# Windowed attention and a gated feed-forward on one core: third tile's units moved, second weight block rebuilt in order of use, first weights behind first transposes

## The chip, the core and the metric

The kernel runs on one core of one Trainium2 chip. The metric is the device time of one execution in microseconds (us). The core's engines work side by side, each through its own row of instructions in order: TensorE (PE for matmuls, PEld for the loading of their stationary operand), VectorE (DVE), ScalarE (ACT), GpSimd (POOL), and SyncE (SP), which here only issues DMAs. They wait for each other by semaphores.

## The reference

```python
pos = np.arange(S)
rel = pos[:, None] - pos[None, :]
mask = (rel >= 0) & (rel < 64)
scores = np.where(mask, q @ k.T / sqrt(D), -1e9)
attn = softmax(scores)
x = heads_side_by_side(attn @ v)
gate = 1.0 / (1.0 + np.exp(-(x @ w_gate)))
val = x @ w_val
out = (gate * val) @ w_out
```

This is the reference in short. Batch 8, 8 heads, 576 positions, head size 64, so 4608 tokens of 512 features; the hidden layer has 1536 features. q, k and v are float32; the three weights come as 64-bit floats and are handed in as 64-bit integers.

## The kernel before, in words

**Tiles.** The tokens are cut into 12 tiles of 384 (`TT`), taken as pairs. An attention *unit* is one tile and one pair of heads, `(t, p)`, and has three stages: `stage_a` (scores s by 24 small matmuls on TensorE, L200; the masked row minimum on VectorE, L218; exponentials on ScalarE, L227; the row sums' reciprocals on VectorE, L233 and L234; the multiplication by them on GpSimd, L236), `stage_b` (transposes pp on TensorE, L244, copied to pT by ScalarE, L249) and `stage_c` (oo = attention times v, L261). A name such as s0_2_0 is half 0 of tile 2, heads pair 0.

**Weights.** A weight block j (128 hidden features) has three pieces: m = 0 gate, m = 1 value, m = 2 output; the piece's number is i = 3j + m. Each is fetched as 64-bit words (`raw`, `conv_load`, L99) and rebuilt: `conv_a` on ScalarE (L111 writes w32, L112 the low part), `conv_b` on VectorE (L120 zz, L122, L124), and `conv_c`, which splits it in two parts whose sum carries nearly all bits, by a cast on ScalarE (L143) and a subtraction on VectorE (L144). Pieces 0 and 1 of a block are also stored to DRAM: w32 itself (w32d, L137) and its parts (wd, L397), for later pairs of tiles. There are 6 buffers for raw, 3 for w32 (`W32`), 7 for the split pieces (`WB`).

**The first pair of tiles.** Tiles 0 and 1 go through the feed-forward directly: ph = up-projection (`up`, L296, 12 matmuls each, gate and value), a sigmoid on ScalarE (L317), the product h and its split on VectorE, and y = down-projection (`down`, L360, 9 matmuls per block of tile 0). Names: ph1_0_2 is the value half (1) of tile 0 in block 2; w1_2 is the piece m = 1 of block 2. During it the units of tiles 2 and 3 are slipped in. Later pairs use a product scheme with seven block products (`product`, L451) and weights read back from DRAM; the change leaves these stages as they are.

**What sets the order.** Python code gives every step a planned time (`put`) and sorts by it (L642); a scheduler then places the instructions on the engines. TensorE keeps the sorted order (`pe`, `keep_in_program_order`). `tc.issue_after` keeps an instruction behind another in the scheduler's order. Exponentials and sigmoids use two different tables of ScalarE; `table_order` chains them in the planned order. `plan` (L532 and on) lists up and down steps of the first pair; position i of it gets, from `fill`, the stages of units: a unit's scores half a position past its start, its transposes some three positions later, its oo at the next start. Before, the starts are 1, 6, 11, 16, ... Conversions get their times at L579, and their `issue_after` marks at L645 to L652.

Of the kernel before, what the change touches and what calls it, by code (L numbers as in the profile page):

```python
# [26 lines left out]
def attn_ffn(ctx: ExitStack, tc: tile.TileContext, qT, kT, vN, w_gate, w_val, w_out, out):  # L27


    nc = tc.nc  # L30
# [4 lines left out]
    NP = DM // P  # L35
# [23 lines left out]
    for key in ((0, 0), (1, 0), (0, 1)):  # L59
        m = const.tile([P, P], F32, name=f"m_{key[0]}{key[1]}")  # L60
        nc.gpsimd.memset(m, 0.0)
        for h in range(2):
            rows = slice(h * BLK, (h + 1) * BLK)
            nc.gpsimd.affine_select(out=m[rows], in_=m[rows], pattern=[[1, P]], compare_op=ALU.is_ge,
                                    fill=NEG, base=-1, channel_multiplier=-1)
            nc.gpsimd.affine_select(out=m[rows], in_=m[rows], pattern=[[-1, P]], compare_op=ALU.is_ge,
                                    fill=NEG, base=BLK, channel_multiplier=1)
            if key[h]:
                nc.gpsimd.affine_select(out=m[rows], in_=m[rows], pattern=[[1, P]], compare_op=ALU.is_ge,
                                        fill=NEG, base=-BLK, channel_multiplier=0)  # L70
# [8 lines left out]
    marks = {"pT": {}}  # L79
# [46 lines left out]
    def conv_c(i):  # L126
        j, m = divmod(i, KINDS)
        _, w32 = conv.pop(i)
        tag, bufs = ("W", WB) if m < 2 else (f"wo_{j}", 1)
        w2 = wts.tile([P, 2, DM], F32R, name=f"w{m}_{j}", tag=tag, bufs=bufs)  # L130
        hi, lo = w2[:, 0, :], w2[:, 1, :]
        split(w32, hi, lo, nc.vector)
        if m == 2:
            wo[j] = (hi, lo)
        else:
            wgv[m][j] = (hi, lo)
            nc.sync.dma_start(out=w32d[m][j], in_=w32)  # L137
            H = DM // 2
            for name, half in (("A11", 0), ("A12", 1)) if j < NK else (("A22", 1),):
                put_part(m, j % NK, name, w2[:, :, half * H:(half + 1) * H])  # L140

    def split(w32, hi, lo, eng):
        nc.scalar.copy(hi, w32)  # L143
        eng.tensor_sub(out=lo, in0=w32, in1=hi.bitcast(F32))  # L144

# [246 lines left out]
    def put_part(m, k, name, parts):  # L394
        n = [w for w, _, _ in PRODUCTS].index(name)
        q, half = divmod(NPR * m + n, 2)
        nc.sync.dma_start(out=wd[k][q][:, half], in_=parts.bitcast(F32))  # L397

    def w_sums(m, k):
        H = DM // 2  # L400
        a1, a2 = [mp.tile([P, DM], F32, name=f"a{i}_{m}_{k}", tag="w32", bufs=W32) for i in range(2)]
        nc.sync.dma_start(out=a1, in_=w32d[m][k])
        nc.sync.dma_start(out=a2, in_=w32d[m][k + NK])
        sw = mp.tile([P, 4, H], F32, name=f"sw_{m}_{k}", tag="raw", bufs=RAW)
        nc.gpsimd.tensor_add(out=sw[:, 0, :], in0=a2[:, :H], in1=a2[:, H:])
        nc.gpsimd.tensor_sub(out=sw[:, 1, :], in0=sw[:, 0, :], in1=a1[:, :H])
        nc.gpsimd.tensor_sub(out=sw[:, 2, :], in0=a1[:, :H], in1=a2[:, :H])
        nc.gpsimd.tensor_sub(out=sw[:, 3, :], in0=a1[:, H:], in1=sw[:, 1, :])
        for i in range(0, 4, 2):
            w2 = wts.tile([P, 2, 2, H], F32R, name=f"ws{i}_{m}_{k}", tag="W", bufs=WB)  # L410
            split(sw[:, i:i + 2, :], w2[:, 0], w2[:, 1], nc.gpsimd)
            for e in range(2):
                put_part(m, k, f"S{i + e + 1}", w2[:, :, e, :])
# [90 lines left out]
    def put(tm, o, f, *a):  # L504
        events.append((tm, o, f, a))
# [24 lines left out]
    def unit(s, n):  # L530
        return 2 * s + n // 2 % 2, n // 4 + n % 2 * 2

    plan, fill = [], {}
# [5 lines left out]
        if n < NF:  # L539
            plan.append(("up", 1, n))  # L540
    at, now = {}, 0.0
    for n in range(2 * NP):
        i = 1 + 5 * n
        fill.setdefault(i + 0.5 + (i < len(plan) and plan[i][0] == "down"), []).append((0, *unit(1, n)))
        late = 0.5 if i + 3 < len(plan) and plan[i + 3][0] == "up" else 1
        for f, d in ((1, 3 + late), (2, 5)):
            fill.setdefault(i + d, []).append((f, *unit(1, n)))

    def attend(i):
        nonlocal now  # L550
# [25 lines left out]
            now = 0.0  # L576
    for i in range(KINDS * NF):
        j, m = divmod(i, KINDS)
        tm = at[("up", 0, max(j, 1))] + ((-10, -2, 10 * j - 5) if j < 2 else (-14, -12, 2))[m]  # L579
        if i < 2:  # L580
            tm = A0 + 11 + 8 * i
        else:
            put(tm - (30 if j == 0 or j == 1 and m < 2 else 6), 2.5, conv_load, i)
        put(tm, 1, conv_a, i)
        put(tm + 2.4, 2, conv_b, i)
        put(tm + 2.5, 2, conv_c, i)
# [20 lines left out]
    for s in range(1, NS):  # L607
        a, b = 2 * s, 2 * s + 1
# [11 lines left out]
        for k in range(NK):  # L620
# [5 lines left out]
            for m in range(2):  # L626
                for n in range(NPR):
                    put(now, 9, product, s, k, m, n)
                    now += PRT
                    if n in (2, 4, 6) and len(downs) > (RESERVE if m else 0) * (k == 1):  # L630
                        j, x = downs.pop(0)
# [11 lines left out]
    for _, _, f, a in events:  # L643
        if f in (conv_a, conv_b, conv_c):
            with ExitStack() as behind:  # L645
                j, m = divmod(a[0], KINDS)
                key = j - AHEAD if m < 2 else j - 1
                early = ("1_2",) if a[0] == 3 else ("1_3",) if a[0] in (2, 4) else (key, "1_3")
                for ins in [i for nm in early for i in marks.get(nm, ())]:
                    behind.enter_context(tc.issue_after(ins))  # L650
                f(*a)
        else:  # L652
            f(*a)
# [43 lines left out]
```

## Time and profile before

| what | us |
|---|---|
| median of 3 runs (1025.39 to 1027.74) | 1027.52 |
| the profiled execution | 1027.02 |
| its span, first to last instruction | 1025.2 |
| PE busy, share of the span | 987.4, 96% |
| DVE busy | 661.5, 65% |
| ACT busy | 525.8, 51% |
| POOL busy | 264.2, 26% |
| granted TensorE clock, mean | 0.997 |

Times in rows of the profile count from the span's start. A row of the timeline has the start, the duration, the engine, the source line, the operation with what it writes and reads (numbers left out), how many it merges, and in brackets how long its engine was idle before it and what ended that. A row of the stretches has for each engine the busy time and the number of instructions, then the granted TensorE clock (1.00 is full speed), the share of the 16 DMA engines and GB/s. A source line of the kernel after is one higher than before from L144 on, and further on by up to four.

### The profile page before, as it was taken

The numbers are of one execution on the slowest core, as the hardware profiler recorded it, in microseconds if no ns is written. First come the engines' busy times: TensorE is split into PE (matmuls) and PEld (weight loads), VectorE is DVE, ScalarE is ACT, GpSimd is POOL, SyncE is SP. The second block draws the span as 40 slices with busy tenths as digits, with TensorE's granted clock in tenths as the row PEclk, the third lists the DMA queues.
The fourth block names the chain that finished last, engine by engine and source line by source line (L and its number), as shares of the span: only waits on it lengthen the run. The fifth ranks groups of instructions, "written<-read, shape, count | busy, mean of one in ns | idle before, by whom it ended". The sixth has DMA issues, their size and how long they took to land.

```text
span 1025.2 us, 19858 instructions
## 1 busy us (share of the span) xinstructions
PE 987.4 (96%) x6984; PEld 883.3 (86%) x6984; DVE 661.5 (65%) x1810; ACT 525.8 (51%) x1409; POOL 264.2 (26%) x287
## 2 busy tenths in 40 slices
PE   6869999998999999999999999999999999999998
PEld 4769999887799888989988989988989988999996
DVE  6878987736676765766665766676666677344532
ACT  6967876736565445544453654454555544311122
POOL 4200101676762241122122221213212124010100
PEclk9989999999999999999999999999999999999999
DMA  9799985989999723767651776761777662466500
GB/s 301 276 312 332 305 301 187 333 301 336 380 323 317 223 96 127 236 211 221 206 184 47 239 230 205 220 203 40 226 221 214 209 194 73 138 221 203 188 31 32
DMA packets 126244, 221.51 MB, mean 216 GB/s; under 512 B 9409, under 2 KB 82625, under 8 KB 126145
## 3 DMA queue, kind: packets, MB, share of 16 engines
q1 hardware_dynamic: 126144, 220.24, 65.9%
q8 instruction: 56, 0.92, 0.4%
q14 instruction: 44, 0.35, 0.1%
HBM read 178.52 MB, written 41.68 MB: 215 GB/s over the span
## 4 chain that ended last, share of the span: by engine, by line
PE 76%; DMA 6%; DVE 6%; ACT 5%; POOL 3%; issue 3%; SPq 0%; POOLq 0%; DVEq 0%; ACTq 0%
PE pr L451 40%; PE y L360 24%; PE ph L296 5%; PE oo L261 3%; PE s L200 3%; PE pp L244 2%; ACT p L227 2%; DVE w L124 1%; POOL ws L144 1%; DMA out_dram<-yo 1%; DVE w L122 1%; DMA raw<-in_moe_w_gate_dram 1%; DVE p L218 1%; DMA k<-in_kT_dram 1%; ACT raw L112 1%
## 5 line engine op out<-in xcount | busy, mean ns | idle before, releaser
L451 PE MATMUL pr<-x_T,wt 128*128 128x384 f32 x1440 | 288.7, 340 | 5.1 <-DVE c L457 2.8
L451 PEld LDWEIGHTS pr<-x_T,wt 128*128 128x128 f32 x1440 | 251.0, 188 | 21.4 <-DVE u L457 5.4
L360 PE MATMUL y<-w,hh 128*128 128x512 f32 x804 | 250.4, 392 | 0.0
L451 PE MATMUL pr<-x_B,wt 128*128 128x384 f32 x1080 | 221.0, 341 | 0.2
L451 PEld LDWEIGHTS pr<-x_B,wt 128*128 128x128 f32 x1080 | 187.9, 188 | 7.9 <-ACT g L306 1.3
L236 POOL TENSOR_TENSOR p<-p,rs 128x384 f32<-128x384 f32 x92 | 78.5, 855 | 407.9 <-DVE rs L234 374.6
L360 PEld LDWEIGHTS y<-w,hh 128*128 128x128 f32 x804 | 148.7, 188 | 21.4 <-ACT hh L325 1.4
L360 PE MATMUL y<-w,hl 128*128 128x512 f32 x402 | 158.6, 394 | 0.6 <-DVE hl L329 0.6
L457 DVE TENSOR_TENSOR u<-pr,p 128x384 f32<-128x384 f32 x120 | 66.7, 556 | 132.0 <-PE pr L451 128.1
L227 ACT ACTIVATE p<-p,mn 128x128 f32<-128x128 f32 x288 | 110.5, 393 | 75.6 <-DVE mn L218 75.4
L329 POOL TENSOR_TENSOR hl<-h,hh 128x384 fp32r<-128x384 f32 x60 | 64.6, 1077 | 239.9 <-DVE hh L327 229.3
L296 PE MATMUL ph<-x,w 128*128 128x384 f32 x576 | 110.3, 344 | 8.5 <-ACT w L143 7.2
L296 PEld LDWEIGHTS ph<-x,w 128*128 128x128 f32 x576 | 100.9, 191 | 12.5 <-ACT w L143 7.8
L360 PEld LDWEIGHTS y<-w,hl 128*128 128x128 f32 x402 | 75.4, 188 | 19.5 <-DVE hl L329 3.3
L218 DVE CUSTOM_DVE_ANT_0 p<-s,m 128x128 f32<-128x128 f32 x288 | 65.3, 286 | 34.9 <-PE s L200 29.3
L462 ACT COPY p<-pr 128x384 f32<-128x384 f32 x60 | 28.4, 473 | 90.5 <-PE pr L451 76.7
L457 DVE TENSOR_TENSOR c<-pr,u 128x384 f32<-128x384 f32 x120 | 66.7, 556 | 12.1 <-PE pr L451 5.8
L249 ACT COPY pT<-pp 128x384 f32<-128x384 f32 x96 | 42.0, 481 | 49.0 <-PE pp L244 48.9
L329 DVE TENSOR_TENSOR hl<-hb,hh 128x384 fp32r<-128x384 f32 x60 | 39.1, 663 | 40.5 <-ACT hh L325 40.1
L310 DVE SCALAR_TENSOR_TENSOR g<-g,e 128x384 f32<-128x384 f32 x96 | 53.3, 567 | 8.0 <-ACT e L307 5.6
L261 PEld LDWEIGHTS oo<-pT,v 128*64 128x64 f32 x1152 | 39.2, 139 | 21.0 <-ACT pT L249 11.4
L325 ACT CAST hh<-hb 128x384 fp32r<-128x384 f32 x60 | 30.0, 512 | 51.6 <-PE y L360 51.4
(73 smaller groups left out, 1221.2 us busy)
## 6 DMA issues: line engine op xcount, KB each, us to landing
wt<-wd SPq DMA_DIRECT2D x210, 512.0 KB, 4.3
v<-in_vN_dram SPq DMA_DIRECT2D x48, 384.0 KB, 4.5
wd<-ws SPq DMA_DIRECT2D x48, 256.0 KB, 4.9
k<-in_kT_dram SPq DMA_DIRECT2D x48, 224.0 KB, 4.1
q<-in_qT_dram SPq DMA_DIRECT2D x48, 192.0 KB, 4.0
wd<-w SPq DMA_DIRECT2D x36, 256.0 KB, 6.2
out_dram<-yo SPq DMA_DIRECT2D x36, 256.0 KB, 2.1
raw<-in_moe_w_gate_dram SPq DMA_DIRECT2D x12, 512.0 KB, 4.6
```

Source lines behind the costliest of these rows:

```text
L200: pe(nc.tensor.matmul(sc[h][half * BLK:(half + 1) * BLK, u, :], qt[h * BLK:(h + 1) * BLK, U * BLK:(U + 1) * BLK], kt[h * BLK:(h + 1) * BLK ...
L218: nc.vector.tensor_tensor_reduce(out=pt[:, u, :], in0=sc[h][:, u, :], in1=masks[key], op0=ALU.add, op1=ALU.min, scale=-SCALE, scalar=3.0e3 ...
L227: exp = nc.scalar.activation(pt[:, u, :], pt[:, u, :], AF.Exp, bias=mn[:, u:u + 1], scale=-1.0, **sums)
L236: eng.tensor_mul(out=pt, in0=pt, in1=rs.unsqueeze(2).broadcast_to([P, UP, P]))
L249: cp = nc.scalar.copy(pT, pp)
L261: pe(nc.tensor.matmul(oo[h * BLK:(h + 1) * BLK, U * BLK:(U + 1) * BLK], vt[:, U, h * BLK:(h + 1) * BLK], pT[h][:, U // 2, half * BLK:(half ...
L296: pe(nc.tensor.matmul(ph, l, r, start=i == 0, stop=i == len(prs) - 1))
L310: nc.vector.scalar_tensor_tensor(out=g, in0=g, scalar=1.0, in1=e, op0=ALU.add, op1=ALU.mult)
L329: return eng.tensor_sub(out=h_lo, in0=h32, in1=h_hi.bitcast(F32))
L360: pe(nc.tensor.matmul(yb[y], l, r, start=first and n == 0, stop=last and n == 2))
L451: pe(nc.tensor.matmul(ps, l, r, start=new and i == 0, stop=i == len(prs) - 1, skip_group_check=not new))
L457: nc.vector.tensor_add(out=o, in0=ps, in1=a)
```

## The change

```diff
-        split(w32, hi, lo, nc.vector)
+        marks[("w", i)] = (split(w32, hi, lo, nc.vector),)
...
     def split(w32, hi, lo, eng):
-        nc.scalar.copy(hi, w32)
+        cp = nc.scalar.copy(hi, w32)
         eng.tensor_sub(out=lo, in0=w32, in1=hi.bitcast(F32))
+        return cp.ins
...
-    for n in range(2 * NP):
-        i = 1 + 5 * n
-        fill.setdefault(i + 0.5 + (i < len(plan) and plan[i][0] == "down"), []).append((0, *unit(1, n)))
-        late = 0.5 if i + 3 < len(plan) and plan[i + 3][0] == "up" else 1
-        for f, d in ((1, 3 + late), (2, 5)):
-            fill.setdefault(i + d, []).append((f, *unit(1, n)))
+    starts = (4, 8, 13, 17, 22, 26, 31, 36, 41)
+    for n, (i, nxt) in enumerate(zip(starts, starts[1:])):
+        late = 0 if nxt < i + 5 else 0.5 if i + 3 < len(plan) and plan[i + 3][0] == "up" else 1
+        for f, x in ((0, i + 0.5), (1, i + 3 + late), (2, nxt)):
+            fill.setdefault(x, []).append((f, *unit(1, n)))
...
-        tm = at[("up", 0, max(j, 1))] + ((-10, -2, 10 * j - 5) if j < 2 else (-14, -12, 2))[m]
+        tm = at[("up", 0, max(j, 1))] + ((-10, -2, 6 * j - 0.5) if j < 2 else (-9, -8, 2) if j == 2 else (-14, -12, 2))[m]
...
-                early = ("1_2",) if a[0] == 3 else ("1_3",) if a[0] in (2, 4) else (key, "1_3")
+                early = {3: ("1_2",), 2: ("1_3",), 4: ("1_3",), 5: ("1_3",)}.get(a[0], (key,))
+                if j == 2 and m < 2:
+                    early += tuple(("w", i) for i in (3, 4))
                 for ins in [i for nm in early for i in marks.get(nm, ())]:
                     behind.enter_context(tc.issue_after(ins))
+                if a[0] < 2:
+                    behind.enter_context(tc.issue_after(marks["pT"][a[0]]))
```

Three things move. The units of tiles 2 and 3 with heads pairs 0 and 2, which are the first four slipped in, start at plan positions 4, 8, 13 and 17 instead of 1, 6, 11 and 16; the first and the third of them have their transposes half a position nearer behind their scores than the others. Block 2's gate and value pieces stand behind the casts of block 1's, so that block 1 (w0_1, w1_1) is rebuilt first, then w2_0, then block 2. And the first two pieces (w0_0, w1_0) are rebuilt only behind the copies of the first and the second unit's transposes. No instruction is added or taken away.

ScalarE at the program's start, before (p are exponentials, pT the copies of transposes, w32, raw and w the steps of a weight piece):

```order
L227 ACTIVATE p0_0_1_305,rs0_0_1_307<-p0_0_1_305,mn0_0_1_306 128x128 x3
L111 ACTIVATE w32_0_0_399<-raw_0_0_224 128x512
L112 ACTIVATE raw_0_0_224<-raw_0_0_224 128x512
L227 ACTIVATE p1_0_1_317<-p1_0_1_317,mn1_0_1_318 128x128 x3
L249 COPY pT0_0_0_352<-pp0_0_0_348 128x384
L143 CAST w0_0_424<-w32_0_0_399 128x512
L249 COPY pT1_0_0_358<-pp1_0_0_354 128x384
L227 ACTIVATE p0_0_2_360,rs0_0_2_362<-p0_0_2_360,mn0_0_2_361 128x128 x3
L227 ACTIVATE p1_0_2_372<-p1_0_2_372,mn1_0_2_373 128x128 x3
L111 ACTIVATE w32_1_0_548<-raw_1_0_233 128x512
```

and of the kernel after:

```order
L228 ACTIVATE p0_0_1_305,rs0_0_1_307<-p0_0_1_305,mn0_0_1_306 128x128 x3
L228 ACTIVATE p1_0_1_317<-p1_0_1_317,mn1_0_1_318 128x128 x3
L250 COPY pT0_0_0_350<-pp0_0_0_346 128x384
L250 COPY pT1_0_0_356<-pp1_0_0_352 128x384
L228 ACTIVATE p0_0_2_358,rs0_0_2_360<-p0_0_2_358,mn0_0_2_359 128x128 x3
L228 ACTIVATE p1_0_2_370<-p1_0_2_370,mn1_0_2_371 128x128 x3
L111 ACTIVATE w32_0_0_397<-raw_0_0_224 128x512
L112 ACTIVATE raw_0_0_224<-raw_0_0_224 128x512
L273 CAST x_0_0_415<-oo_0_0_402 128x384
L250 COPY pT0_0_1_434<-pp0_0_1_430 128x384
L143 CAST w0_0_422<-w32_0_0_397 128x512
L250 COPY pT1_0_1_440<-pp1_0_1_436 128x384
```

The three steps of w0_0 that stood ahead of and between the copies pT0_0_0 and pT1_0_0 now follow the exponentials of the third unit; the cast of w0_0 stands between the copies of the second unit.

ScalarE at the second block, before, from the exponentials of the unit (2, 0) to the cast of w1_1:

```order
L227 ACTIVATE p0_2_0_909,rs0_2_0_911<-p0_2_0_909,mn0_2_0_910 128x128 x3
L227 ACTIVATE p1_2_0_921,rs1_2_0_923<-p1_2_0_921,mn1_2_0_922 128x128 x3
L143 CAST w0_2_976<-w32_0_2_933 128x512
L111 ACTIVATE w32_1_1_964<-raw_1_1_418 128x512
L111 ACTIVATE w32_1_2_969<-raw_1_2_875 128x512
L317 ACT_TABLE_LOAD
L317 ACTIVATE g_0_1_995<-ph0_0_1_982 128x384
L112 ACTIVATE raw_0_3_1036<-raw_0_3_1036 128x512
L112 ACTIVATE raw_1_3_1053<-raw_1_3_1053 128x512
L111 ACTIVATE w32_2_1_1046<-raw_2_1_967 128x512
L112 ACTIVATE raw_2_2_1070<-raw_2_2_1070 128x512
L143 CAST w1_1_1001<-w32_1_1_964 128x512
```

and after, from the first step of w1_1 on:

```order
L111 ACTIVATE w32_1_1_907<-raw_1_1_400 128x512
L112 ACTIVATE raw_1_1_400<-raw_1_1_400 128x512
L111 ACTIVATE w32_2_0_912<-raw_2_0_428 128x512
L112 ACTIVATE raw_2_0_428<-raw_2_0_428 128x512
L112 ACTIVATE raw_2_1_910<-raw_2_1_910 128x512
L318 ACTIVATE g_1_0_880<-ph0_1_0_867 128x384
L143 CAST w0_1_845<-w32_0_1_838 128x512
L143 CAST w1_1_940<-w32_1_1_907 128x512
L112 ACTIVATE raw_0_2_882<-raw_0_2_882 128x512
L112 ACTIVATE raw_1_2_884<-raw_1_2_884 128x512
L143 CAST w2_0_950<-w32_2_0_912 128x512
L111 ACTIVATE w32_0_2_972<-raw_0_2_882 128x512
```

The two steps of w1_1 now stand ahead of w2_0's and the gate g_1_0, its cast right behind w0_1's; the table loads and the exponentials of the unit have left this place, and block 2's w32 steps follow w2_0's cast.

TensorE from the up half ph0_1_0 to the transposes of the unit (2, 0), one row or two of each step, before:

```order
L296 MATMUL ph0_1_0_877<-x_1_3_862,w0_0_424 128x384 x3
L200 MATMUL s0_2_0_895<-k_2_0_839,q_2_0_838 64x128
L200 MATMUL s1_2_0_896<-k_2_0_839,q_2_0_838 64x128
...
L296 MATMUL ph1_1_0_943<-x_1_3_862,w1_0_583 128x384 x3
L296 MATMUL ph0_0_1_982<-x_0_0_415,w0_1_869 128x384 x3
...
L296 MATMUL ph1_0_1_1017<-x_0_0_415,w1_1_1001 128x384 x3
...
L360 MATMUL y_0_2_1049<-w2_0_940,hl_0_0_807 128x512
L296 MATMUL ph0_1_1_1055<-x_1_0_708,w0_1_869 128x384 x3
...
L244 MATMUL pp0_2_0_1079<-ident_81,p0_2_0_909 128x128 x3
L244 MATMUL pp1_2_0_1085<-ident_81,p1_2_0_921 128x128 x3
L296 MATMUL ph1_1_1_1091<-x_1_0_708,w1_1_1001 128x384 x3
```

and after:

```order
L297 MATMUL ph0_1_0_867<-x_1_3_864,w0_0_422 128x384 x3
L297 MATMUL ph1_1_0_886<-x_1_0_708,w1_0_583 128x384 x3
...
L297 MATMUL ph0_0_1_915<-x_0_0_415,w0_1_845 128x384 x3
...
L361 MATMUL y_0_2_1001<-w2_0_950,hl_0_0_807 128x512
L297 MATMUL ph0_1_1_1017<-x_1_0_708,w0_1_845 128x384 x3
...
L201 MATMUL s0_2_0_1041<-k_2_0_935,q_2_0_934 64x128
L201 MATMUL s1_2_0_1042<-k_2_0_935,q_2_0_934 64x128
...
L297 MATMUL ph1_1_1_1079<-x_1_0_708,w1_1_940 128x384 x3
...
L361 MATMUL y_0_2_1001<-w2_1_1038,hl_0_1_969 128x512
L245 MATMUL pp0_2_0_1183<-ident_81,p0_2_0_1055 128x128 x3
L245 MATMUL pp1_2_0_1189<-ident_81,p1_2_0_1067 128x128 x3
```

The scores s_2_0 moved from behind ph0_1_0 to behind ph0_1_1, past four up halves and a y; the transposes pp moved from behind ph0_1_1 to behind the y of block 1.

## The prediction

> **What bounds the kernel now.** I read the page first, then busy time by stretch, then TensorE's waits, then the timelines of the engines around the one large gap. TensorE leads:
>
> ```profile
> PE 987.4 (96%) x6984; PEld 883.3 (86%) x6984; DVE 661.5 (65%) x1810; ACT 525.8 (51%) x1409; POOL 264.2 (26%) x287
> ```
>
> So 1025.2 - 987.4 = 37.8 us without a matmul is all that any reordering can win, beside matmuls that ran slowly. By stretch (columns: us, busy us and instructions of PE, PEld, DVE, ACT, POOL, then granted clock, DMA share, GB/s), the one big gap lies between 52 and 61 us, and the clock is granted at half speed just behind it:
>
> ```profile
> 52.00:61.00 9.00, 2.18 (x11) 1.86 (x12) 7.72 (x17) 8.92 (x24) 2.19 (x2) 0.89 0.91 301
> 61.00:62.00 1.00, 0.80 (x3) 0.29 (x3) 1.00 (x3) 0.37 (x1) 0.00 (x0) 0.50 1.09 262
> 62.00:66.00 4.00, 4.00 (x12) 3.91 (x13) 2.24 (x4) 2.11 (x4) 0.00 (x0) 0.52 0.88 263
> ```
>
> TensorE's timeline through it (L200 scores, L296 up-projection; the y rows are L360, from the chain in order of time; the bracket is the idle time before the row and what ended it):
>
> ```profile
> 46.79 0.89 PE L200 MATMUL s<-k,q 64*64 64x128 f32 x24
> 47.60 2.38 PE L296 MATMUL ph<-x,w 128*128 128x384 f32 x12
> 50.34 0.62 PE L296 MATMUL ph<-x,w 128*128 128x384 f32 x2 [0.35 <-ACT w L143]
> 51.94 2.01 PE L296 MATMUL ph<-x,w 128*128 128x384 f32 x10 [0.98 <-DVE w L144]
> 60.77 1.01 PE L296 MATMUL ph<-x,w 128*128 128x384 f32 x2 [6.82 <-ACT w L143]
> 61.98 3.57 PE L296 MATMUL ph<-x,w 128*128 128x384 f32 x10 [0.20 <-DVE w L144]
> 70.34 6.50 PE L296 MATMUL ph<-x,w 128*128 128x384 f32 x36
> 116.43 0.91 PE L261 MATMUL oo<-pT,v 128*64 128x64 f32 x22 [0.47 <-ACT pT L249]
> ```
>
> ```profile
> 65.55 2.29 PE y L360 x9
> 89.34 2.08 PE y L360 x9
> ```
>
> The rows before order print name them: s_2_0, ph1_1_0, ph0_0_1 (waits for w0_1, 0.35 and 0.98 us), ph1_0_1 (waits for w1_1, 6.82 and 0.20 us), y of block 0. From 62 us on TensorE hardly stops: the 0.47 us of the last row are its only wait until 180 us. The 6.82 us are w1_1's place in ScalarE's row: its conversion starts behind a table load, six exponentials, w0_2, and behind it another table load and a gate stand before its cast:
>
> ```profile
> 50.83 1.28 ACT L227 ACT_TABLE_LOAD   x1
> 52.12 0.40 ACT L227 ACTIVATE p<-p,mn 128x128 f32<-128x128 f32 x1
> 54.95 1.23 ACT L111 ACTIVATE w<-raw 128x512 f32<-128x512 f32 x2
> 56.20 1.28 ACT L317 ACT_TABLE_LOAD   x1
> 60.10 1.27 ACT L143 CAST w<-w 128x512 fp32r<-128x512 f32 x2
> ```
>
> **The second block in order of use.** I replay ScalarE and VectorE from 45 us with the durations of these rows, in the times of the profile before:
>
> ```profile
> 45.35 0.68 ACT L111 ACTIVATE w<-raw 128x512 f32<-128x512 f32 x1
> 49.31 0.47 ACT L317 ACTIVATE g<-ph 128x384 f32<-128x384 f32 x1
> 47.05 2.36 ACT L112 ACTIVATE raw<-raw 128x512 int32<-128x512 uint32 x4
> 46.10 0.68 DVE L124 CUSTOM_DVE_ANT_0 w<-raw,w 128x1024 uint16<-128x1024 uint16 x1
> 46.70 0.91 DVE L120 TENSOR_SCALAR zz<-w 128x512 int32<-128x512 int32 x2
> 47.52 1.29 DVE L122 SCALAR_TENSOR_TENSOR w<-w,zz 128x512 int32<-128x512 int32 x2
> 51.20 0.69 DVE L144 TENSOR_TENSOR w<-w,w 128x512 fp32r<-128x512 f32 x1
> 51.80 0.55 DVE L335 TENSOR_TENSOR h<-ph,g 128x384 f32<-128x384 f32 x1
> ```
>
> Start to start, zz costs 0.41, L122 0.60, L124 0.60, L144 about 0.60, h 0.47; on ScalarE L111 and L112 0.57 each, a cast 0.52. ScalarE from 45.35: w32_1_1, raw_1_1, w32_2_0, raw_2_0, raw_2_1 end at 48.2; gate g_1_0 at 48.7; cast of w0_1 at 49.2. VectorE from 46.70: two zz, two L122, two L124, h32_1_0, then w0_1's subtraction: 0.82 + 1.20 + 1.20 + 0.47 + 0.60 = 4.3, so 51.0, and 51.1 with a semaphore; w1_1's follows at 51.6, w2_0's (a cast of hh between) at 52.6.
>
> TensorE: s_2_0 (0.81, start to start) is gone from here, so ph1_1_0 ends at 49.99 - 0.81 = 49.18. The first two matmuls of ph0_0_1 end at 49.8; it waits 1.3 us for 51.1, then 2.01 to 53.1; ph1_0_1 finds w1_1 ready, 6.50 / 3 = 2.17 to 55.3; y finds w2_0 ready, 2.08 to 57.4. Before, y ended at 65.55 + 2.29 = 67.84: 10.4 us earlier, less the 0.8 of scores that come later: **-9.6 us**. As a check by kind: waits 8.35 to 1.3 give 7.05; slow clock gives 3.57 - 2.01, 1.01 - 0.62 and 2.29 - 2.08 = 2.16; one restart less gives 0.46.
>
> The clock part rests on the rows at 0.50 and 0.52, about 5 us long after a wait of 6.82 us, while the wait of 0.98 us left its ten matmuls at 2.01. So the new wait of 1.3 us should cost no clock. The Trainium skill, "TensorE: Matmul & The Clock Gate", Part 1, says that an idle window of about 3.4 us drops the clock to half and that about 3.4 us of work restore it; by that the slow clock would cost 1.7 us, not 2.16, and the sum would be 0.5 us smaller. The trace's stretch at half clock is longer than the page's, and I use the trace.
>
> **The third tile's units, later.** The four moved units keep all their work: no instruction is added, the table loads stay 18 in ScalarE's row. What can newly be late is the first unit. Its scores now start close behind the second block, at about 59.6, and stand three up halves and one y ahead of pp_2_0 (3 x 2.17 + 2.08 = 8.6 us), while ScalarE puts two weight steps between its two halves. The nearest unit of before, and the stores on which a w32 buffer waits (3 buffers, L106):
>
> ```profile
> 81.99 0.89 PE L200 MATMUL s<-k,q 64*64 64x128 f32 x24
> 89.24 0.83 POOL L236 TENSOR_TENSOR p<-p,rs 128x384 f32<-128x384 f32 x1 [0.74 <-DVE rs L234]
> 91.26 0.82 PE L244 MATMUL pp<-ident,p 128*128 128x128 f32 x6
> L137 SPq DMA_DIRECT2D w32d<-w x16: 319/327/362, 24.1 to 119.5; - x16
> DMA to landing us min/median/max: 2.1/3.8/8.1
> 55.00 2.19 POOL L236 TENSOR_TENSOR p<-p,rs 128x384 f32<-128x384 f32 x2 [14.71 <-DVE rs L234]
> ```
>
> There the second multiplication ended at 90.07, 1.2 us before it was needed. Now: w32_1_2 waits for the store of w32_1_1 (issued at 49.5, landed 3.8 later, 53.3), is written at 53.9, and VectorE's zz, two L122 and one L124 finish w32_0_2 at 56.1; its store lands at 60.0; only then w32_0_3 (60.6), the cast of w2_1 (61.1), the table (62.4), three exponentials at 0.39 (63.6), w32_1_3 and w32_2_2 (64.7), three more (65.9). VectorE, in its own row, has two zz, two L122, two L124, a cast, w0_3's subtraction, hl_1_1 and small ones between w32_1_3 (64.1) and the second reciprocal, 5.1 us: 69.2. GpSimd's 0.83 to 1.1 us end at 70.1 to 70.3. TensorE is there at 57.4 + 2.17 + 0.82 + 8.6 = 69.0, its first three transposes end at 69.4: **+0.9 us**. Ends: 0 by the row of 91.26; with one store at 8.1 instead of 3.8, 4.3 more, 5.2. I take 0.9, near the median landing.
>
> Cover elsewhere: behind 56.1 VectorE has zz, L124, h, L122 and w0_2's subtraction (58.8), then a cast and w1_2's (59.8); they are wanted at 62.6 and 64.7, so 3.8 us cover them; this cover also hides the moved SP order (raw_1_2 and the wd stores of block 0 move behind a store; q_2_2 and k_2_2 move back, wanted only at 79). raw_1_6 now queues on SP behind k_3_0, which waits for s_2_2, at about 79; block 6 is wanted past 110. From the fifth unit on the row of TensorE is the same, so what is won by then stays.
>
> The Trainium skill, "ScalarE: Activation LUTs", section "What ACT_TABLE_LOAD costs", speaks against putting a table load in front of this unit: 2.66 us with its drain. The trace has 1.28 us at 50.83 and the next exponential at 52.12, so no drain shows; by the page the wait at pp_2_0 would be 1.4 us longer and the sum 1.4 us smaller.
>
> **First weights behind first transposes.** Before, ScalarE waited in order for the first raw weights, and the transposes' copies stood behind that:
>
> ```profile
> 12.94 0.67 ACT L111 ACTIVATE w<-raw 128x512 f32<-128x512 f32 x1 [1.84 <-DMA raw<-in_moe_w_gate_dram]
> 16.05 0.62 ACT L143 CAST w<-w 128x512 fp32r<-128x512 f32 x1 [0.66 <-DVE w L124]
> 13.63 0.43 DVE L120 TENSOR_SCALAR zz<-w 128x512 int32<-128x512 int32 x1 [2.12 <-ACT w L111]
> 24.00:28.00 4.00, 2.79 (x54) 1.94 (x46) 3.97 (x21) 4.00 (x15) 1.78 (x3) 1.00 1.13 365
> 28.00:32.00 4.00, 2.76 (x55) 2.06 (x55) 3.96 (x26) 4.00 (x16) 2.36 (x3) 1.00 1.02 382
> ```
>
> The waits go, but ScalarE and VectorE are full from 24 to 32 us, so only idle time that is not given back counts. By the same durations ScalarE, free of the wait at 12.94 - 1.84 = 11.1, reaches the cast of w0_0 at about 17.0 and there waits for VectorE's L124 until about 18.5, with pT1_0_1 queued behind it and oo_0_1 waiting for that: 1.5 to 2 of its 1.84 + 0.66 come back. Gain between 0 and VectorE's 2.12 us; I take **-0.8**, nearer the low end because of that cast.
>
> Sum: -9.6 + 0.9 - 0.8 = -9.5. The profiled execution took 1027.02, 0.5 under the median of 1027.52; the median becomes 1018.0.
>
> **The rivals.** *More comes through*: no wait at pp_2_0 and all of 2.12 at the start: -11.7, 1015.8. For it the row of 91.26; against it ScalarE's order. *DMA takes part of it back*:
>
> ```profile
> q1 hardware_dynamic: 27921, 36.33, 91.1%
> ```
>
> In the first 120 us the DMA engines are busy for 109.3 us, and 9.5 us less leaves 98.9%. If 95% is the most that can be had, 115.1 us are needed, only 4.9 are won: 1022.6. Against it: the stretch 61 to 62 stands at 1.09 without a wait for data. *Slower*: the w32 stores. ScalarE runs in order, so a late store holds exponentials, gates and casts together. If stores land at 8.1, the first unit waits 5.2 us and, past a wait of some 3 us, loses 2.2 of clock; the third unit (8.6 us too) the same: 14.8 against 10.4 won, 4.4 slower, 1031.9. It decides when two such waits pass 3 us each, landings of about 5.9 for both. For it: the DMA share above; against: 3.8 in the median. *The change doesn't do what it says*: the wait moves from w1_1 to w0_1 and w2_0, if VectorE takes the third block's steps first; the new rows have them behind, so little is left for it; 1027.
>
> **How the numbers follow.** Forecast 0.62, more 0.15, DMA 0.13, slower 0.05, nothing 0.05. The range of 1015.0 to 1023.0 takes in the first three cases. A difference of 0.3%, 3.1 us, is what a measurement of this kernel can tell. Faster by more 0.88 (the first three, less 0.02 for the tail of DMA's), within it 0.07, slower 0.05.
>
> **What would show it.** Right: no wait over 2 us for L143 between 45 and 66 us, granted clock 1.00 there, y of block 0 ending near 57 (56.6 with the start's gain), a wait for GpSimd under 2 us at pp_2_0, and later stages shifted as a whole. Wrong: a wait of over 3 us for w0_2, w2_1 or pp_2_0, a granted clock under 0.9 after 20 us, or ScalarE waiting for w32d stores in unit after unit.

## The result and the profile after

| | before | after |
|---|---|---|
| median of 5 runs each, us | 1027.74 (1025.39 to 1030.44) | 1020.06 (1018.96 to 1021.63) |
| the profiled execution | 1027.02 | 1020.06 |
| its span | 1025.2 | 1018.3 |
| mean granted clock | 0.997 | 0.994 |

The ratio of after to before is 0.9925, 95% interval 0.9904 to 0.9945: faster by 7.7 us in the medians, 6.9 us in the spans of the two profiled executions, where the prediction had 9.5. TensorE still leads; the time without a matmul fell from 37.8 us to 1018.3 - 985.9 = 32.4 us:

```profile
PE 985.9 (97%) x6984; PEld 883.3 (87%) x6984; DVE 662.8 (65%) x1810; ACT 525.8 (52%) x1409; POOL 265.7 (26%) x287
```

TensorE's timeline of the kernel after, through the second block to the first unit's transposes and, in the last row, to the scores of the fifth unit (L297 is the up-projection, L361 y, L245 pp, L201 s):

```profile
48.15 0.61 PE L297 MATMUL ph<-x,w 128*128 128x384 f32 x2 [0.27 <-ACT w L143]
50.07 5.66 PE L297 MATMUL ph<-x,w 128*128 128x384 f32 x22 [1.31 <-DVE w L144]
...
57.42 0.39 PE L361 MATMUL y<-w,hl 128*128 128x512 f32 x1
57.65 2.27 PE L297 MATMUL ph<-x,w 128*128 128x384 f32 x12
...
69.12 0.49 PE L245 MATMUL pp<-ident,p 128*128 128x128 f32 x3
72.42 0.55 PE L245 MATMUL pp<-ident,p 128*128 128x128 f32 x3 [2.81 <-POOL p L237]
...
136.46 0.89 PE L201 MATMUL s<-k,q 64*64 64x128 f32 x24
```

The waits of 6.82 and 0.20 us for w1_1 are gone, w2_0 is not waited for, and the wait for w0_1 is 1.31 us. Two things are longer than forecast: the 22 matmuls behind that wait (5.66 us), and the wait for GpSimd at pp_2_0 (2.81 us). The fifth unit's scores began at 143.18 us before, so 6.7 of the 6.9 us are there by then; what comes later is shifted as a whole. That row of before:

```profile
143.18 0.89 PE L200 MATMUL s<-k,q 64*64 64x128 f32 x24
```

By stretch (the same columns as in the prediction), the clock behind the wait of 1.31 us is at half speed for about 3.4 us (0.34 us of the first row, all of the second, 0.08 us of the third):

```profile
50.00:51.00 1.00, 0.93 (x4) 0.93 (x5) 1.00 (x4) 1.00 (x3) 0.00 (x0) 0.83 0.81 258
51.00:54.00 3.00, 3.00 (x11) 3.00 (x11) 2.87 (x7) 2.28 (x5) 0.00 (x0) 0.50 0.88 279
54.00:55.00 1.00, 1.00 (x7) 1.00 (x6) 1.00 (x4) 0.26 (x1) 0.00 (x0) 0.96 1.03 370
```

For the wait at pp_2_0 I follow p backwards. SyncE issues the store of a w32 half; ScalarE waits for it ahead of w32_0_3, and with it wait the table load and the six exponentials behind:

```profile
55.60 0.33 SPq L137 DMA_DIRECT2D w32d<-w  x1
```

```profile
59.96 0.49 ACT L318 ACTIVATE g<-ph 128x384 f32<-128x384 f32 x1 [1.39 <-PE ph L297]
61.40 0.68 ACT L111 ACTIVATE w<-raw 128x512 f32<-128x512 f32 x1 [0.95 <-DMA w32d<-w]
...
62.60 1.28 ACT L228 ACT_TABLE_LOAD   x1
63.90 0.40 ACT L228 ACTIVATE p<-p,mn 128x128 f32<-128x128 f32 x1
...
66.96 0.39 ACT L228 ACTIVATE p<-p,mn 128x128 f32<-128x128 f32 x1
67.25 0.19 ACT L228 ACTIVATION_READ_ACCUMULATOR p<-p,mn 128x1 f32 x1
```

From its issue to the end of the wait are 61.40 - 55.60 = 5.8 us; the prediction had put in 3.8. But an earlier store would have gained only the 0.95 us of this wait: the gate ahead of it ended at 60.45, since it had waited 1.39 us for ph0_1_1, which the half clock had made late. The sums of the second half are there at 67.44. VectorE needs them for the addition L234 and the reciprocal L235, but has weight steps in its row ahead of each:

```profile
67.09 0.99 DVE L328 CAST hh<-h 128x384 fp32r<-128x384 f32 x1
68.00 0.68 DVE L122 SCALAR_TENSOR_TENSOR w<-w,zz 128x512 int32<-128x512 int32 x1
68.60 0.15 DVE L234 TENSOR_SCALAR rs<-rs 128x3 f32<-128x3 f32 x1
68.67 0.68 DVE L122 SCALAR_TENSOR_TENSOR w<-w,zz 128x512 int32<-128x512 int32 x1
69.27 0.68 DVE L144 TENSOR_TENSOR w<-w,w 128x512 fp32r<-128x512 f32 x1
69.87 0.54 DVE L330 TENSOR_TENSOR hl<-h,hh 128x384 fp32r<-128x384 f32 x1
70.34 0.68 DVE L124 CUSTOM_DVE_ANT_0 w<-raw,w 128x1024 uint16<-128x1024 uint16 x1
70.94 0.16 DVE L235 RECIPROCAL rs<-rs 128x3 f32<-128x3 f32 x1
```

```profile
67.03 0.83 POOL L237 TENSOR_TENSOR p<-p,rs 128x384 f32<-128x384 f32 x1 [27.82 <-DVE rs L235]
71.28 1.09 POOL L237 TENSOR_TENSOR p<-p,rs 128x384 f32<-128x384 f32 x1 [3.42 <-DVE rs L235]
```

Of the 4.9 us from the sums (67.44) to p (72.37), 3.5 are VectorE's row. Not all of that is order: the cast hh at its head took 0.99 us beside GpSimd's first multiplication, where the four others of this trace between 40 and 75 us took 0.35 or 0.36.

### The profile page after: what moved, and what is told of

It reads as the page before. It is cut to its first block, busy times and chain, and to the rows that moved or that the text cites. A ratio compares the mean times of both kernels' runs of the same rounds, so it can differ in the third digit from the quotient of the medians.

```text
span 1018.3 us, 19859 instructions
## 1 busy us (share of the span) xinstructions
PE 985.9 (97%) x6984; PEld 883.3 (87%) x6984; DVE 662.8 (65%) x1810; ACT 525.8 (52%) x1409; POOL 265.7 (26%) x287
## 4 chain that ended last, share of the span: by engine, by line
PE 75%; DVE 7%; DMA 7%; ACT 5%; issue 2%; POOL 2%; SPq 0%; POOLq 0%; DVEq 0%; ACTq 0%
PE pr L452 40%; PE y L361 23%; PE ph L297 4%; PE oo L262 3%; PE s L201 3%; ACT p L228 2%; PE pp L245 2%; DMA wt<-wd 1%; DMA a<-w32d 1%; DVE w L124 1%; DMA w32d<-w 1%; DVE p L219 1%; DMA out_dram<-yo 1%; DVE w L122 1%; DMA hd<-hh 1%
## 5 line engine op out<-in xcount | busy, mean ns | idle before, releaser
L361 PE MATMUL y<-w,hh 128*128 128x512 f32 x804 | 250.0, 392 | 0.0
L361 PEld LDWEIGHTS y<-w,hh 128*128 128x128 f32 x804 | 148.6, 188 | 21.3 <-ACT hh L326 1.4
L361 PE MATMUL y<-w,hl 128*128 128x512 f32 x402 | 158.6, 395 | 0.7 <-DVE hl L330 0.7
L330 POOL TENSOR_TENSOR hl<-h,hh 128x384 fp32r<-128x384 f32 x60 | 64.6, 1076 | 240.1 <-DVE hh L328 231.2
L297 PE MATMUL ph<-x,w 128*128 128x384 f32 x576 | 109.6, 343 | 1.7 <-DVE w L144 1.3
L297 PEld LDWEIGHTS ph<-x,w 128*128 128x128 f32 x576 | 100.8, 191 | 4.9 <-DVE w L144 1.6
L361 PEld LDWEIGHTS y<-w,hl 128*128 128x128 f32 x402 | 75.3, 187 | 19.5 <-DVE hl L330 3.4
L330 DVE TENSOR_TENSOR hl<-hb,hh 128x384 fp32r<-128x384 f32 x60 | 39.1, 663 | 40.5 <-ACT hh L326 40.0
L274 DVE TENSOR_TENSOR x_T<-t,x_T 128x384 fp32r<-128x384 f32 x40 | 39.3, 999 | 27.1 <-ACT x_T L273 27.1
```

The lines of the kernel that those rows point to most:

```text
L274: lo = eng.tensor_sub(out=x2[:, 1, :], in0=src, in1=x2[:, 0, :].bitcast(F32))
L297: pe(nc.tensor.matmul(ph, l, r, start=i == 0, stop=i == len(prs) - 1))
L330: return eng.tensor_sub(out=h_lo, in0=h32, in1=h_hi.bitcast(F32))
L361: pe(nc.tensor.matmul(yb[y], l, r, start=first and n == 0, stop=last and n == 2))
```

## The experiments

The theory after the result: the shortfall is the half clock behind the wait of 1.31 us (about 1.5 us) and the 1.9 us by which pp_2_0 waits longer than forecast, which comes from ScalarE's waits for stores. The rivals: the half clock belongs to the execution and not to the wait; and the wait at pp_2_0 comes from VectorE's row. Each kernel was run in 5 rounds beside the kernel before; three groups of four kernels, each on one chip, with medians of before of 1027.31, 1027.41 and 1026.90 us.

**The three parts apart.** `start_only` is before with the last edit alone, `order_only` after without the units' move and without the start, `units_only` before with the units' move alone, `no_start` after without the start, and `order_start` after without the units' move.

The start's lines, added to before in `start_only`, taken from after in `no_start` and `order_only`:

```diff
+                if a[0] < 2:
+                    behind.enter_context(tc.issue_after(marks["pT"][a[0]]))
```

The units' positions, put back in `order_only` and `order_start` (in `units_only` before has those of after):

```diff
-    starts = (4, 8, 13, 17, 22, 26, 31, 36, 41)
...
+    for n in range(2 * NP):
+        i = 1 + 5 * n
...
```

> The kernel before, with the third part of the change alone (first weights behind first transposes). Theory (the start's gain is a shift of 1.07 us that nothing later takes back, since the wait for w1_1 hangs on ScalarE's row behind x_1_3, which shifts with it): span 1024.1, 1.0 to 1.2 us under the kernel before, the 6.82 us wait for w1_1 unchanged within 0.3. Rival (the start's gain is absorbed by the wait for w1_1, as a fixed time of data landing): no change of the span, the wait grown by about 1 us.

> The kernel before, with the second block rebuilt in order of use and block 2 behind it, but the third tile's units at their old places and the start as before. Theory (the gap came from the order of conversions alone; the move of the units is what brings the wait at pp_2_0): the 6.82 us wait is gone, a first wait of at most 1.5 us for w0_1 stays, pp_2_0 waits for nothing, 7.5 to 9.6 us under the kernel before: better than the whole change without its start. Rival (the exponentials and two table loads that now stand ahead of w2_0 and block 2 on ScalarE make those late): waits of 3 to 5 us for w2_0 or w0_2, gain under 5 us.

> The kernel before, with the first four units of the third and fourth tile later, and the conversions and the start as before. Theory: w1_1 still stands behind w2_0 and w0_2 on ScalarE, but two table loads and six exponentials (about 5 us) are out of its way: the wait of 6.82 us shrinks to 2 to 4 us, the wait at pp_2_0 is under 1 us since VectorE's reciprocals come before block 4's steps; gain 3 to 6 us. Rival (the conversion order is all): wait for w1_1 over 5 us, gain under 2 us.

> The changed kernel without its third part (first weights as before). Theory (parts are additive): 1.07 us over the changed kernel, 5.8 us under the kernel before in span, with the waits of about 1.3 us for w0_1 and 2.8 us at pp_2_0 both there. Rival (the wait at pp_2_0 and the slow clock behind the first wait come and go with the phase of what runs before): the wait at pp_2_0 is under 1.5 us or the granted clock stays at 1.00, and this kernel is as fast as the changed one.

> The kernel after with the third tile's units at their old positions: the order of conversions and the start, without the units' move. Theory (the order carries the gain, the start its 1.1 us of shift, the units' move nothing): 1020 within 1, and a wait for GpSimd of about 2.5 us at pp_2_2 in the place of that at pp_2_0. Rival (the move is worth what it took off the kernel before, 1.8 us): 1022 or more.

| kernel | median, us | ratio to before | scores of the fifth unit at | ph0_0_0 at |
|---|---|---|---|---|
| start_only | 1027.07 | 1.0001 [0.9986, 1.0016] | 142.08 | 35.72 |
| units_only | 1025.74 | 0.9983 [0.9972, 0.9995] | 140.77 | 36.57 |
| order_only | 1020.85 | 0.9944 [0.9925, 0.9962] | 137.63 | 36.63 |
| no_start (order and units) | 1021.94 | 0.9951 [0.9934, 0.9968] | 137.96 | 36.71 |
| order_start | 1020.57 | 0.9936 [0.9916, 0.9955] | 137.98 | 37.07 |
| after (all three) | 1020.06 | 0.9925 [0.9904, 0.9945] | 136.46 | 35.75 |

The order of conversions carries most of it: alone, by the ratios, 5.8 of the 7.7 us, and its interval overlaps that of after. The units' move alone is worth about 1.8 us, and on top of the order nothing that can be measured. Both fell short of their theories (7.5 to 9.6 us and 3 to 6 us). The reason stands in three rows. Alone, it takes the wait for w1_1 only from 6.82 to 4.20 us, and the clock, granted at 0.50 from 52 to 61 us, is still half behind it (TensorE's timeline of `units_only`):

```profile
58.09 4.08 PE L296 MATMUL ph<-x,w 128*128 128x384 f32 x12 [4.20 <-ACT w L143]
```

And with the order alone, the wait for GpSimd doesn't exist at pp_2_0 but at pp_2_2, nearly as long as the one of after (TensorE's timeline of `order_only`; `order_start` has 2.49 us there too, at 85.57):

```profile
51.73 4.09 PE L297 MATMUL ph<-x,w 128*128 128x384 f32 x22 [1.64 <-DVE w L144]
...
85.22 0.56 PE L245 MATMUL pp<-ident,p 128*128 128x128 f32 x3 [2.49 <-POOL p L237]
```

So the move shifts the late softmax from one unit to another. The first of these rows is against the theory on the clock: a wait of 1.64 us, and the 22 matmuls behind take 4.09 us, at full speed. So is the first row here, of `no_start`, behind the same wait as in after; its wait at pp_2_0 is longer than in after, and there the clock falls (0.50 from 73.31 to 76.72 us):

```profile
51.02 4.11 PE L297 MATMUL ph<-x,w 128*128 128x384 f32 x22 [1.29 <-DVE w L144]
...
72.36 0.55 PE L245 MATMUL pp<-ident,p 128*128 128x128 f32 x3 [3.35 <-POOL p L237]
```

**Filling the wait.** Nine transposes that nobody uses, between ph1_1_0 and ph0_0_1.

```diff
...
+            if (t, j) == (0, 1):
+                put(now, 8.9, fill_pe, 9)
             put(now, 9, up_gate, t, j)
```

> The kernel after with nine transposes of the identity put on TensorE between ph1_1_0 and ph0_0_1, where it waits 1.31 us for VectorE; their result is used by nobody, so this kernel computes nothing less. Theory (the wait of 1.31 us drops the clock to half for some 3 us, which costs 1.4 us): the transposes take about 1.2 us and lie in the wait, the 22 matmuls behind take 4.1 us instead of 5.5 at a clock of 1.00 in 51 to 54 us, y of block 0 ends at about 56.3 instead of 57.65, and the time is about 1.4 us under the kernel after: 1018.6 against 1020.06, ratio to the kernel before 0.991. Rival (the half clock belongs to the run and not to the wait): a stretch of half clock of about 3 us stands within 48 to 60 us all the same, or none stood there in most runs anyway, and the time stays within 0.7 us of 1020.06.

1018.97 us, ratio 0.9916 [0.9897, 0.9935]. TensorE's timeline:

```profile
50.09 4.08 PE L297 MATMUL ph<-x,w 128*128 128x384 f32 x22 [0.85 <-DVE w L144]
...
70.62 0.55 PE L245 MATMUL pp<-ident,p 128*128 128x128 f32 x3 [2.57 <-POOL p L237]
```

The clock held and the time is where the theory put it, but after `no_start` this doesn't decide: the clock may have held without the filling. The interval overlaps that of after.

**Scores in the wait.** The 24 score matmuls of s_2_0 behind ph1_1_0.

```diff
+            if (t, j) == (0, 1):
+                put(now - LOAD_AHEAD, 8, load_qk, 2, 0)
+                put(now - LOAD_AHEAD, 8.5, load_v, 2, 0)
+                put(now, 8.9, scores, 2, 0)
+                now += APT[0]
...
+            if (f, t, p) == (0, 2, 0):
+                put(now, 6, softmax, t, p)
+                continue
```

> The kernel after with the 24 score matmuls of s_2_0 (0.89 us) put behind ph1_1_0, into the wait of 1.31 us ahead of ph0_0_1; the softmax stays at its place. Theory: the wait shrinks to about 0.4 us, the clock holds at 1.00 behind it, block 0's y ends at about 56.3 and everything behind the scores' old place comes 0.9 + 1.4 us earlier: about 2 us under the kernel after, 1018. Rival: q and k of this unit land too late or the two exps that now stand together ahead of w32_0_3 on ScalarE hold up its casts, and a wait of 1 to 2 us for w0_2 or w1_2 behind y of block 0 takes the gain: 1019.5 to 1021.

1018.28 us, ratio 0.9911 [0.9891, 0.9930]. The wait ahead of ph0_0_1 fell to 0.83 us and the clock held; pp_2_0 waits for nothing, but y of block 1 now waits for w2_1, since the six exponentials stand together ahead of w32_0_3, as the rival had it for other pieces:

```profile
37.65 2.35 PE L297 MATMUL ph<-x,w 128*128 128x384 f32 x12
...
51.96 4.09 PE L297 MATMUL ph<-x,w 128*128 128x384 f32 x22 [0.83 <-DVE w L144]
...
68.12 0.50 PE L361 MATMUL y<-w,hh 128*128 128x512 f32 x1 [1.41 <-DVE w L144]
```

The first row is ph0_0_0, 1.9 us later than in after although nothing ahead of it on TensorE was edited. A stretch of this execution says why: the clock fell at another place.

```profile
29.00:37.00 8.00, 6.65 (x66) 4.88 (x67) 6.18 (x36) 5.54 (x20) 3.84 (x5) 0.57 1.04 390
```

**Four buffers for w32.** Paid for with one buffer instead of two for the tile e.

```diff
-    RAW, W32 = 6, 3
+    RAW, W32 = 6, 4
...
-        e = mp.tile([P, TT], F32, name=f"e_{nm}", tag="e", bufs=2)
+        e = mp.tile([P, TT], F32, name=f"e_{nm}", tag="e", bufs=1)
```

> The kernel after with four buffers for the halves w32 instead of three, and one buffer instead of two for the tile e of the hidden activation, which pays for it in memory. Theory (the wait of 2.81 us at pp_2_0 comes from ScalarE's waits of 0.48 and 0.95 us for stores of w32d): these waits go, the exps of unit 2_0 end about 1.4 us earlier, the wait at pp_2_0 is about 1.4 us, and the time is 1 to 1.5 us under the kernel after. Rival (the wait at pp_2_0 is set by what stands ahead of the reciprocal on VectorE, which ran from 67.34 to 70.94 us behind the exps): the stores' waits go and the wait at pp_2_0 stays over 2.3 us, time within 0.7 us of 1020.06. If the single tile e costs, waits for e at the activations of the hidden stage show it.

1030.89 us, ratio 1.0038 [1.0024, 1.0053]. The single tile e costs more than all the rest: in the later stages (from 250 us on, by line) TensorE waits 8.4 us for the gate and VectorE 13.9 for e, where after has 0.1 and 1.7.

```profile
L452 PE MATMUL pr<-x_B,wt 128*128 128x384 f32 x1038 | 212.9, 341 | 8.4 <-ACT g L307 8.4
L311 DVE SCALAR_TENSOR_TENSOR g<-g,e 128x384 f32<-128x384 f32 x92 | 52.2, 567 | 17.1 <-ACT e L308 13.9
```

Ahead of that, the first unit's wait of 2.81 us shrank to 0.94 and 0.55 us, one ahead of each half's transposes, and the fifth unit's scores came at 134.08, 2.4 us earlier than in after (1.6 of it because the clock held behind the wait of 1.30 us). The sum, 1.5 us, is about what the theory said, but it did not come about as the theory had it: ScalarE still waits 1.77 us for a store.

```profile
60.61 0.66 ACT L111 ACTIVATE w<-raw 128x512 f32<-128x512 f32 x1 [1.77 <-DMA w32d<-w]
```

What changed is VectorE's row: the scheduler had put the second reciprocal 1.0 us behind its addition (66.79 and 67.79), against 2.3 in after (68.60 and 70.94). That points to the rival.

**The transposes half a position later.**

```diff
-        late = 0 if nxt < i + 5 else 0.5 if i + 3 < len(plan) and plan[i + 3][0] == "up" else 1
+        late = 0.5 if n == 0 else 0 if nxt < i + 5 else 0.5 if i + 3 < len(plan) and plan[i + 3][0] == "up" else 1
```

> The kernel after with the transposes of the third tile's first unit half a position later, between ph0_1_2 and ph1_1_2. Theory (ScalarE's late exps and VectorE's row set when GpSimd's p is there, at 72.4 us, whatever TensorE does): TensorE has 12 matmuls or about 2.1 us more to do ahead of pp_2_0, whose wait shrinks from 2.81 to about 0.7 us, and the time is up to 2.1 us lower, 1018 to 1019. Rival (the wait moves on): the wait appears at pp_2_1 or pp_2_2, as it stood at pp_2_2 with 2.49 us in the kernel with the order alone, or at w0_3 and w1_3, and the time is within 0.7 us of 1020.06.

1017.26 us, ratio 0.9906 [0.9884, 0.9928]. The wait at pp_2_0 shrank from 2.81 to 1.15 us and came up nowhere else before 170 us as one wait. But the second unit's scores came 3.3 us earlier than in after (76.94 against 80.21) and the fifth's only 2.25 (134.21 against 136.46): 1.0 us is lost again on the way, in pieces of 0.3 to 0.4 us from unit to unit. Again the clock held behind the wait of 1.29 us:

```profile
50.00 4.08 PE L297 MATMUL ph<-x,w 128*128 128x384 f32 x22 [1.29 <-DVE w L144]
...
71.23 0.55 PE L245 MATMUL pp<-ident,p 128*128 128x128 f32 x3 [1.15 <-POOL p L237]
```

**VectorE's row.** Without the addition, the reciprocal takes its place in the row, three weight steps and the split of h (L330) earlier. This kernel leaves the small term out for one unit.

```diff
-            nc.vector.tensor_scalar_add(out=rs, in0=rs, scalar1=1e-9)
+            if (t, p) != (2, 0):
+                nc.vector.tensor_scalar_add(out=rs, in0=rs, scalar1=1e-9)
```

> The kernel after without the addition of 1e-9 to the sums of the softmax of the third tile's first unit; so this kernel leaves out that small term there. On VectorE the reciprocal of the unit's second half then stands where the addition stood: behind one L122 and ahead of the next L122, hl, L144 and L124 (0.68 + 0.68 + 0.54 + 0.68 us). Theory (VectorE's row holds up p, whose sums were there at 67.44 us while the reciprocal ran at 70.94): GpSimd's second multiplication begins about 2.4 us earlier, the wait of 2.81 us at pp_2_0 shrinks to about 0.4, and the time is up to 2.4 us under the kernel after: about 1018. Rival (ScalarE's waits for stores and pieces set it): the wait stays over 2 us and the time within 0.7 us of 1020.06.

1017.52 us, ratio 0.9908 [0.9889, 0.9927]; span 1014.5. TensorE's timeline (lines are one higher in this kernel), with VectorE's reciprocal and GpSimd's multiplication behind it:

```profile
50.03 5.65 PE L298 MATMUL ph<-x,w 128*128 128x384 f32 x22 [1.30 <-DVE w L144]
...
69.07 0.82 PE L246 MATMUL pp<-ident,p 128*128 128x128 f32 x6
69.64 4.42 PE L298 MATMUL ph<-x,w 128*128 128x384 f32 x24
```

```profile
67.27 0.16 DVE L236 RECIPROCAL rs<-rs 128x3 f32<-128x3 f32 x1
```

```profile
67.60 1.10 POOL L238 TENSOR_TENSOR p<-p,rs 128x384 f32<-128x384 f32 x1 [2.35 <-DVE rs L236]
```

This execution is the best twin of after: up to 69 us the same TensorE rows within 0.05 us, half clock and all. The wait at pp_2_0 is gone. The sums were there at 66.32 (no store was waited for in this execution), 1.1 us earlier, and the reciprocal followed them by 0.95 us instead of 3.50. So of the 3.7 us by which the reciprocal came earlier, 2.55 are VectorE's row and 1.1 the store. With the shorter row alone, behind the sums of after, p would be there 2.4 us after 67.44, at 69.8, against 69.6 when TensorE wants it: 0.2 us of wait. With the earlier sums alone, 4.93 us after 66.32, at 71.25: 1.6 us. These two are estimates, which let each part shift by itself; by them both causes are real, and the row is the larger one.

**Both moves together** (`combo`: the edits of `scores_early` and `pp_late`).

> The kernel after with both moves: the 24 score matmuls of s_2_0 in the wait ahead of ph0_0_1, and the transposes of this unit half a position later. Theory (the two shortfalls add): no wait over 1 us ahead of y of block 0 and none at pp_2_0, 1016 to 1017. Rival: pp_2_0 waited for nothing with the early scores (its p was there at 66.4 us), and the wait of 1.41 us for w2_1 at block 1's first y stays; so the second move adds nothing and the time is that of the early scores, 1018.3 within 0.7.

1017.44 us, ratio 0.9898 [0.9876, 0.9919]: between the two expectations. Its trace is the rival's: nothing is waited for at pp_2_0, and the wait for w2_1 stays.

```profile
67.67 0.50 PE L361 MATMUL y<-w,hh 128*128 128x512 f32 x1 [1.41 <-DVE w L144]
```

**The first pieces later still.** Behind the second and the third unit's transposes.

```diff
-            tm = A0 + 11 + 8 * i
+            tm = A0 + 15 + 8 * i
...
-                    behind.enter_context(tc.issue_after(marks["pT"][a[0]]))
+                    behind.enter_context(tc.issue_after(marks["pT"][a[0] + 1]))
```

> The kernel after with the first pieces of the expert weights converted one unit later, behind the second and third unit's transposes. Theory (ScalarE's wait of 1.84 us for VectorE at w0_0 holds up pT1_0_1 and makes oo_0_1 wait 2.51 us, behind which the clock is half in 20 to 23 us): this wait goes, the clock is 1.00 in 20 to 24, the first matmuls of the hidden stage begin up to 1 us earlier, at about 35, if the weights are there; 1 us under the kernel after, 1019. Rival (the pieces are the longer way): ph0_0_0 waits for w0_0 at 36 us for over 1 us, and the time is 1 us above, 1021.

1020.54 us, ratio 0.9937 [0.9920, 0.9955]. Both were wrong on the mechanism. A wait of 3.37 us for VectorE came up ahead of the scores, and yet ph0_0_0 began at 35.79, as in after, and waited for no weight:

```profile
21.84 1.56 PE L201 MATMUL s<-k,q 64*64 64x128 f32 x24 [3.37 <-DVE w L124]
...
34.57 1.29 PE L262 MATMUL oo<-pT,v 128*64 128x64 f32 x24 [0.29 <-ACT pT L250]
```

What TensorE loses at 17 to 24 us, by waits or by a half clock, is slack: it waits again at 30 to 35 us. The start is held by something common to these kernels that I didn't single out.

## Why the prediction was right, and where its sum was off

**The bound** was right: TensorE's row, and in it the place of w1_1's cast in ScalarE's. `order_only` shows that it was the order of conversions that won most of it.

**The second block, -9.6.** The replay held: the wait for w0_1 was forecast at 1.3 us and measured at 1.31, w1_1 and w2_0 were ready. The step that failed is "the new wait of 1.3 us should cost no clock", argued from a wait of 0.98 us that had cost none. In the profiled execution of after it cost 5.66 - 4.08 = 1.6 us, by the row of `pp_late`, and y ended at 57.65 instead of 56.6; the term became -8.0. This cost isn't one of the kernel alone but of the execution. Six profiled executions of different kernels have that wait at 1.29 to 1.31 us: three were followed by half clock (after, `no_eps`, `start_later`), three were not (`no_start`, `w32_4`, `pp_late`). Behind 1.60 and 1.64 us none of two were, behind 0.82 to 0.85 none of three. That the wait makes such a stretch possible is likely; that filling it prevents the stretch isn't shown.

The stretches themselves say what differs. Apart from the one at the program's end, each lasts 3.41 us or a multiple of it, and the two of after begin at 19.94 and 50.66 us, nine times 3.41 apart. Counted in such steps from a stretch of the same trace, the step ahead of the fall in after holds both waits for w0_1, 0.27 and 1.31 us; in `pp_late` it begins behind the shorter one:

```profile
47.25:50.66 3.41, 1.83 (x9) 1.20 (x8) 3.41 (x7) 3.13 (x7) 0.00 (x0) 1.00 0.93 282
50.66:54.07 3.41, 3.41 (x13) 3.41 (x12) 3.28 (x8) 2.69 (x5) 0.00 (x0) 0.50 0.91 288
```

```profile
48.07:51.48 3.41, 2.10 (x10) 1.78 (x11) 3.41 (x8) 3.17 (x6) 0.00 (x0) 1.00 0.92 306
```

TensorE was busy for 1.82 to 1.84 us of that step in the three executions where the clock fell, and for 1.90 (`w32_4`), 2.10 (`pp_late`) and 2.12 (`no_start`) in the three where it held. So whether this wait costs the clock seems to hang on where it lies in the steps, which no edit here sets. It is argued from these rows and not tested, and the busy time is no sharp limit: in before, TensorE was busy for 1.73 us from 52.22 to 55.64, and the clock held in the step behind.

The Trainium skill, "TensorE: Matmul & The Clock Gate", Part 1, says that the clock is judged in windows of about 3.4 us that run freely, not from the kernel's start, so that the cold stretch varies from run to run. The steps of 3.41 us and the three of six agree with that. That it takes an idle window of that length doesn't agree: after 1.31 us of idle time the clock was at half. The prediction read the stretch of before as longer than the one of the Trainium skill; it lasted 6.83 us from 59.05, which is two windows, and in the first of them TensorE stood idle until 60.77.

**The third tile's units, +0.9.** Mis-sized: 2.81 us. TensorE came to the second three transposes at 69.6 (forecast 69.4), and the reciprocal followed the exponentials by 3.5 us (forecast 3.3), but the exponentials ended at 67.44 instead of 65.9: one store landed after 5.8 us where I had put the median of 3.8, which cost 1.0 to 1.1 us by the wait of 0.95 us and by `no_eps`, and the rest is the gate that the half clock made late; GpSimd took 1.09 behind a gap of 0.2. It stayed within the bounds of 0 and 5.2. I had priced VectorE's row and not asked whether it need be so long: with the reciprocal where the addition stood, the wait is gone. The table load ahead of the exponentials took 1.28 us from 62.60, and the first exponential started at 63.90, 0.02 us behind it, so the longer wait wasn't its doing. The drain of the Trainium skill, "ScalarE: Activation LUTs", section "What ACT_TABLE_LOAD costs", doesn't show here either.

**The start, -0.8.** ph0_0_0 began 1.06 us earlier in after and 1.09 in `start_only`. The cast of w0_0 did hold up pT1_0_1, and TensorE waited 2.51 us for it at 19.65, which then cost nothing. But the medians of `start_only` (ratio 1.0001) don't show the gain, and with the order of conversions in place the intervals with and without the edit overlap (0.9936 against 0.9944, 0.9925 against 0.9951). Of ten profiled executions with this edit, seven had ph0_0_0 at 35.70 to 35.79, and three (`scores_early`, `combo`, `order_start`) at 37.07 to 37.65, each with half clock somewhere in 29 to 37 us; the four without the edit had it at 36.57 to 36.81. Whether the edit makes those stretches more frequent, four executions can't tell, and it stays open.

**The sum** for the profiled execution: -9.6 + 1.6 + 2.8 - 1.1, less the 0.47 us that TensorE waited at 116 us before and doesn't now, is -6.8; the spans differ by 6.9.

**Its signs and its rivals.** Of the signs that the prediction named, two went against it: the clock fell under 0.9 after 20 us, and the wait at pp_2_0 was over 2 us. The forecast held within its range because these two errors, 1.6 and 1.9 us, fit into it. More didn't come through, by the same two. The wait didn't move on to w0_1: 1.31 us there, as replayed. That DMA takes part of it back, with 95% as the most to be had, is refuted: the DMA engines' share from 0 to 110 us went from 0.92 to 0.97. The one on the slower side had the right mechanism, a late store that reaches pp_2_0, but 5.8 us for one store instead of 8.1 for two, and it decided nothing.

**Faster versions.** With all of the reference computed, `pp_late` (0.9906) and `combo` (0.9898) are the fastest here. The intervals overlap that of after (0.9925), so that they beat it isn't shown by the times. Nor do the traces show it for `pp_late`: of the 2.25 us that it is ahead at the fifth unit's scores, 1.6 are the clock, and only about 0.7 is left of the wait at pp_2_0 that is 1.7 us shorter.

## What to carry to other kernels

When a gap is caused by the order in which an engine works off its row, put that row in the order of use first: here it was worth about 5.8 of 7.7 us, and moving the consumers away from the gap only moved the wait to another of them. Price a moved step by the latest landing of the stores ahead of it, not by their median, and look at how long finished sums lie in another engine's row: a few small instructions placed between weight steps held up TensorE by more than the store did, as estimated above. Count on a few us of half clock that fall at different places in different executions, some of them where they cost nothing.

## What the runs showed of the hardware

- The granted clock fell to half for 3.41 us or multiples of it (6.83 us in before), behind an idle time of 1.31 us in one execution, and not behind 1.64 us in another. In 20 to 24 us, behind the same instructions, it was 0.58 in after and 1.00 in `fill`.
- GpSimd's multiplication of p takes 0.83 us or 1.09 us; in after, the longer one at 71.28 to 72.37 lay beside VectorE's L124, L336 and L144. The shorter one at 67.03 to 67.86 lay beside the cast hh, which took 0.99 us instead of 0.35.
- Six stores of w32d, 256 KB each, between 40 and 75 us of after landed after times that differ twofold; the longest is the one that ScalarE waited for:

```profile
DMA to landing us min/median/max: 2.7/4.0/5.7
```
